# A matmul with 2:4-pruned weights: the first seven token tiles as runs of 128 neighbouring rows

## The chip, the core and the metric

The kernel runs on one core of a Trainium2 chip. Its matrix unit is TensorE (PE in the profile, with PEld for its weight loads); elementwise work is shared by VectorE (DVE), ScalarE (ACT) and GpSimd (POOL). Transfers are carried out by 16 DMA engines and are started by instructions on queues, here those of SyncE (SP) and of ScalarE. The metric is the device time of one execution in microseconds, as the median of several runs.

## The reference

x has 16 x 512 tokens of 1024 features, w is 1024 x 1024, b has 1024 entries; all are bfloat16. In every column of w, of each four neighbouring rows the two with the larger magnitude stay and the others become zero. Then x is multiplied by the pruned w, and b is added:

```python
wg = w.reshape(G, M, D)                  # M = 4
mag = jnp.abs(wg)
order = jnp.argsort(mag, 1)
thr = jnp.take_along_axis(mag, order[:, M - N:M - N + 1, :], 1)   # N = 2
mask = (mag >= thr)
wp = (wg * mask).reshape(D, D)
return jnp.einsum("bsd,df->bsf", x, wp) + b
```

## The kernel before

The 8192 tokens are 64 tiles of 128. For a tile, TensorE needs x with features on the partitions and tokens along the free dimension, as the stationary operand, and multiplies it with 512 columns of pruned weights at a time; eight blocks of 128 features are summed in one PSUM bank.

The weights are pruned on the chip. w_sb holds w in a layout in which one partition has the four rows of a group of four (w row g\*512 + 4q + m is at partition q, half g, slot m), so that VectorE can compare the four slots. Six pieces are pruned one after another: four of 256 columns of the upper half of the features (pieces 0 to 3), then two of 512 columns of the lower half (4, 5). The result is wp. For most tiles it is then spread by DMAs within the chip into wp_nat, where feature rows lie in their natural order (function spread, tokens W in the orders).

While that goes on, the first seven tiles (NPK = 7) are started early. Their upper 512 features (HK) are loaded untransposed by load_x (lines 105 to 110), in three transfers named by GROUPS: tile 6 alone on ScalarE's queue, tiles 3 to 5 and then 0 to 2 on SyncE's. TensorE transposes them against an identity (function transpose, line 198; in each tile four transposes, for the features of slot m), ScalarE copies the result to xt (line 203), and mm_piece (line 228) multiplies it with the pieces 0 to 3 of wp as they become ready. In these seven tiles a row on partition p and tile t of a group that starts at tile a is row a\*128 + 3p + t of x: function tokens gives that view, and three neighbouring rows of x are on one partition.

The lower 512 features of tiles 0 to 5 come later through two transposing DMAs into xlow (load_low, line 236). These take the 384 rows of a group in natural order, so the columns of a tile are every third one of xlow: the view xq. The sums of the upper half wait in a staging buffer st, to which GpSimd adds the bias; close then multiplies the lower half (function nat, line 242), VectorE adds st (line 429) and writes to o, and a store goes to the rows that rows names. Tiles 7 to 11 (xlead) and all later ones (xb, in batches of up to eight tiles) arrive by transposing DMAs and need neither the on-chip transposes nor tokens.

The order of work on each engine at the start is written out by hand in the table order, one list for each engine (T: transposes of a tile, C: copy, M: matmuls of a tile with a piece, S and U: staging copies, W, X, Y, Z: transfers, A and E: openings of later tiles). On TensorE all seven T stand ahead of the first M, in the order 6, 5, 3, 4, 2, 0, 1. On SyncE's queue the transfers of the start stand in this order: two slots of piece 0 of w; x tiles 3 to 5; x tiles 0 to 2; pieces 1, 2 and 3 of w; the first half of the lower w; then the transposing load of xlead. ScalarE's queue issues the other two slots of piece 0 and tile 6.

Of the kernel before, what the change touches and what calls it, by code (L numbers as in the profile page):

```python
# [10 lines left out]
def kernel(  # L11
# [8 lines left out]
    P = 128  # L20
# [14 lines left out]
    HK = D // G  # L35
    assert G == 2 and Dout == 2 * FH and HK == 512
    xf = x.flatten_outer_dims()
    of = out.flatten_outer_dims()

    NPK = 7  # L40
# [3 lines left out]
    GROUPS = ((0, 3), (3, 6), (6, 7))  # L44
# [21 lines left out]
    def seq(eng, inst):  # L66
        if eng in tails:
            tc.add_manual_dep(inst.ins, tails[eng].ins.name, NOSYNC, reason="program order")
        tails[eng] = inst
        return inst  # L70
# [10 lines left out]
    def sp(i):  # L81
        return seq("sp", i)
# [7 lines left out]
    wv = w.rearrange("(g q m) f -> q g m f", g=G, m=4)  # L90
    x_sb = {}
    
    def tokens(dram, t):
        a, b_ = next(s for s in GROUPS if s[0] <= t < s[1])
        return dram[a * P:b_ * P].rearrange("(p t) k -> p t k", p=P), t - a
    bias_sb = const.tile([P, Dout], bf16)

    def issue(eng, out_, in_):
        q = nc.sync if eng == "sp" else nc.scalar
        return seq(eng, q.dma_start(out_, in_))  # L100
# [3 lines left out]

    def load_x(ta, tb, eng="sp"):
        xs = const.tile([P, tb - ta, HK], bf16, name=f"x_{ta}")
        xv, n = tokens(xf, ta)
        issue(eng, xs[:], xv[:, n:n + tb - ta, :HK])
        for t in range(ta, tb):
            x_sb[t] = xs[:, t - ta, :]  # L110

# [10 lines left out]
    load_w(0, 0, 256, 0, 2)  # L122
    load_w(0, 0, 256, 2, 4, "act")
    load_x(SOLO, SOLO + 1, "act")
    act(nc.scalar.activation(spark[:], nc.const_aps.tensor(1.0, [P, 1], bf16), Act.Abs))
    load_x(3, 6)
    load_x(0, 3)
    load_w(0, 256, 512)
    load_w(0, 512, 768)
# [103 lines left out]
    def load_low(u):  # L233
        a, b_ = GROUPS[u]
        xlow = const.tile([P, 4, (b_ - a) * P], bf16, name=f"xlow{u}")
        sp(nc.sync.dma_start_transpose(out=xlow[:], in_=xf[a * P:b_ * P, HK:]))
        xq = xlow[:].rearrange("p k (q t) -> p k q t", t=b_ - a)
        return {a + t: xq[:, :, :, t] for t in range(b_ - a)}

    def nat(xt, ps, c0, c1, k0=0, k1=KT, first=0, last=KT - 1, koff=0):  # L240
        for kt in range(k0, k1):
# [48 lines left out]
    p = {}  # L290
# [53 lines left out]
    def emit(eng, tok):  # L344
# [10 lines left out]
        elif tok[0] == "Z":  # L355
            load_w(1, 512, 1024)
            sp(nc.sync.dma_start(bias_sb[:], b.partition_broadcast(P)))
        elif tok[0] == "X":
            xnat.update(load_lead(int(tok[1:])))
        elif tok[0] == "Y":  # L360
            xnat.update(load_low(int(tok[1:])))
        elif tok[0] == "E":
            open_solo(int(tok[1:]))
        elif tok[0] == "U":
            t, h = map(int, tok[1:].split("h"))
            stage((t, "h", h))
        elif tok[0] == "A":
            open_nat(*map(int, tok[1:].split("h")))
        elif tok[0] == "C":
            copy_xt(int(tok[1:-1]))  # L370
        elif tok[0] == "M":
            mm_piece(*map(int, base[1:].split(".")), part[k])
        elif tok[0] == "S":
            stage(tuple(map(int, tok[1:].split("b"))))
        else:
            i = int(base[-1])
            if i not in p:
                p[i] = Piece(i)
            if eng == "act":
                p[i].abs_act()  # L380
            else:
                p[i].do(base[:-1], part[k], half.get(k, slice(0, 2)))
# [47 lines left out]
                                        ps.rearrange("p (n c) -> p n c", n=2), add, op=Alu.add))  # L430

    def rows(t):
        if t < NPK:
            ov, n = tokens(of, t)
            return ov[:, n, :]
        return of[t * P:(t + 1) * P, :]

    def store(eng, t, o, c0=0, c1=Dout):
        issue(eng, rows(t)[:, c0:c1], o[:, c0:c1])
# [25 lines left out]
    for bi, (tb, nb) in enumerate(batches):  # L465
        if bi:
            load_batch(bi + 1)
        for j in range(nb):
            t = tb + j
# [49 lines left out]
```

## Time and profile before

| | |
|---|---|
| median of 3 runs | 234.71 us (234.15 to 235.56) |
| the profiled execution | 236.29 us |
| its span, first to last instruction | 234.5 us |
| its mean granted TensorE clock | 0.993 |
| DMA packets, bytes | 79260, 38.19 MB |
| x tiles 0 to 5, untransposed | two transfers of 384 KB |

The page gives busy times of the engines and the chain of work that ended last, followed back from the last instruction. Views of the trace give the chain's pieces in order of time (start, length, what), who waited for whom, groups of instructions with their count and mean duration, and busy times in stretches that one can choose. In the timeline a line gives start, length, engine, line of the kernel, operation, tiles and count. SPq and ACTq are the issuing instructions on the queues; a DMA's own time runs from its issue to its landing.

### The profile page before, as it was taken

To read this page: it belongs to the slowest core of one execution; us is meant where nothing else is said; L and a number is where in the kernel's file an instruction comes from. 1 tells how busy PE (TensorE), PEld (TensorE's weight loads), DVE (VectorE), ACT (ScalarE), POOL (GpSimd) and SP (SyncE) were. 2 spreads that over 40 slices of the span, in tenths; PEclk is the share of its full clock that TensorE was granted. 3 is DMA by queue.
4 is the path that set the end of the run, shared out by engine and by line. 5 is a ranking of instruction groups with operands and counts; after the bars stand their busy time and mean duration, and the time that the engine had idled before them with its cause. 6 is when DMAs were issued, how large, how long until landed. Compare 5 with 4: busy or idle time off the path is not lost.

```text
span 234.5 us, 2804 instructions
## 1 busy us (share of the span) xinstructions
PE 227.3 (97%) x1124; PEld 111.6 (48%) x1144; DVE 107.8 (46%) x191; ACT 14.4 (6%) x27; POOL 17.6 (7%) x15
## 2 busy tenths in 40 slices
PE   6799999999999999999999999999999999999995
PEld 3688444444444444444444444444444444444443
DVE  4599957882442442343344244234334324423434
ACT  3575200000000000000000000000000000000000
POOL 1000079900000000000000000000000000000000
PEclk9799999999999999999999999999999999999999
DMA  5988999997279312992219912594227931222122
GB/s 151 291 171 241 245 189 232 272 327 265 89 168 306 129 69 89 192 282 108 92 59 260 262 63 74 127 307 149 92 89 159 285 137 60 77 89 89 48 89 89
DMA packets 79260, 38.19 MB, mean 163 GB/s; under 512 B 64144, under 2 KB 71696, under 8 KB 79248
## 3 DMA queue, kind: packets, MB, share of 16 engines
q1 hardware_dynamic: 68464, 20.88, 41.6%
q10 hardware_dynamic: 10784, 17.14, 20.5%
q8 instruction: 9, 0.15, 0.3%
q14 instruction: 3, 0.02, 0.0%
HBM read 3.28 MB, written 16.78 MB: 86 GB/s over the span
## 4 chain that ended last, share of the span: by engine, by line
PE 95%; DMA 3%; issue 1%; SPq 0%; DVE 0%
PE ps L242 87%; PE ps L228 5%; DMA x<-in_x_dram 3%; PE tp L242 2%; SPq L100 0%; PE tp L198 0%; PE ps L198 0%; DVE o L427 0%
## 5 line engine op out<-in xcount | busy, mean ns | idle before, releaser
L242 PE MATMUL ps<-wp_nat,xb 128*128 128x512 bf16 (+1 forms) x831 | 178.9, 375 | 0.9
L242 PEld LDWEIGHTS <-xb 128*128 128x128 bf16 x848 | 82.4, 98 | 97.5
L427 DVE TENSOR_TENSOR o<-ps,bias_sb 128x512 bf16<-128x512 f32 (+1 forms) x112 | 71.5, 676 | 114.5 <-PE ps L242 112.2
L423 POOL TENSOR_TENSOR st<-st,bias_sb 128x1024 f32<-128x1024 f32 x8 | 16.7, 2124 | 0.0
L242 PE MATMUL ps<-wp_nat,xlead 128*128 128x512 bf16 x63 | 14.7, 379 | 0.1
L242 PEld LDWEIGHTS <-xlead 128*128 128x128 bf16 x88 | 8.6, 98 | 10.2
L228 PE MATMUL ps<-wp,xt 128*128 128x256 bf16 x112 | 12.7, 277 | 0.0
L429 DVE TENSOR_TENSOR o<-ps,st 128x512 bf16<-128x512 f32 x16 | 11.1, 691 | 2.8 <-PE ps L242 2.0
L228 PEld LDWEIGHTS <-xt 128*128 128x128 bf16 x112 | 11.2, 100 | 1.4
L242 PE MATMUL ps<-wp_nat,xlow 128*128 128x512 bf16 x47 | 10.6, 379 | 0.1
L264 ACT COPY st<-ps 128x512 f32<-128x512 f32 x14 | 7.3, 596 | 3.9 <-PE ps L228 3.8
L242 PEld LDWEIGHTS <-xlow 128*128 128x128 bf16 x48 | 5.0, 103 | 5.4
L162 DVE TENSOR_TENSOR wp<-w_sb,mag 128x256 bf16<-128x256 bf16 (+2 forms) x13 | 6.1, 480 | 0.1
L162 DVE TENSOR_TENSOR mag<-mag,hi 128x256 bf16<-128x256 bf16 (+2 forms) x13 | 6.0, 482 | 0.2
L242 PE MATMUL tp<-wp_nat,xlead 128*128 128x512 bf16 x23 | 5.8, 379 | 0.0
L172 DVE TENSOR_SCALAR mag<-w_sb 128x512 uint16<-128x512 uint16 (+2 forms) x5 | 2.3, 476 | 6.0 <-DMA w_sb<-in_w_dram 6.0
L198 PE MATMUL tp<-ident,x 128*128 128x128 bf16 x20 | 2.4, 283 | 2.6 <-DMA x<-in_x_dram 2.6
L141 PE MATMUL ps<-const-bfloat16-1.0 128*128 128x128 bf16 (+1 forms) x20 | 3.8, 366 | 0.8 <-PEq L503 0.8
L198 PEld LDWEIGHTS <-x 128*128 128x128 bf16 x28 | 2.6, 138 | 3.0 <-DMA x<-in_x_dram 3.0
L141 PEld LDWEIGHTS <-const-bfloat16-1.0 128*128 128x128 bf16 x20 | 1.9, 126 | 2.4 <-issue 2.4
L162 DVE TENSOR_TENSOR lo<-mag 128x512 bf16<-128x512 bf16 (+1 forms) x6 | 3.1, 509 | 0.1
L162 DVE TENSOR_TENSOR hi<-mag 128x512 bf16<-128x512 bf16 (+1 forms) x6 | 3.0, 508 | 0.1
(18 smaller groups left out, 17.1 us busy)
## 6 DMA issues: line engine op xcount, KB each, us to landing
out_dram<-o ACTq DMA_DIRECT2D x58, 256.0 KB, 2.0
wp_nat<-wp SPq DMA_DIRECT2D x14, 128.0 KB, 3.3
out_dram<-o ACTq DMA_DIRECT2D x10, 128.0 KB, 1.7
w_sb<-in_w_dram SPq DMA_DIRECT2D x2, 512.0 KB, 6.0
x<-in_x_dram SPq DMA_DIRECT2D x2, 384.0 KB, 6.3
w_sb<-in_w_dram SPq DMA_DIRECT2D x3, 256.0 KB, 7.1
bias_sb<-in_b_dram SPq DMA_DIRECT2D x1, 256.0 KB, 4.2
wp_nat<-wp ACTq DMA_DIRECT2D x2, 128.0 KB, 3.1
```

Of the source, the lines that this page charges most:

```text
L141: pe(nc.tensor.matmul(warm_ps[:, :rep * P], lhsT=nc.const_aps.tensor(1.0, [P, P], bf16), rhs=nc.const_aps.tensor(1.0, [P, rep * P], bf16), ...
L162: dve(nc.vector.tensor_tensor(out, a, b_, op=op))
L172: dve(nc.vector.tensor_single_scalar(self.mag[:, ms, :].bitcast(u16), self.w[:, ms, :].bitcast(u16), 0x7FFF, op=Alu.bitwise_and))
L198: pe(nc.tensor.transpose(tp[:, m, :], xg[:, m, :], ident[:]))
L228: pe(nc.tensor.matmul(ps[:, c0 + d:c1 + d], lhsT=xpk[t][:, m, :], rhs=wp[:, g, m, c0:c1], start=(new and m == ms.start), stop=(left[key] = ...
L242: pe(nc.tensor.matmul(ps, lhsT=xt[:, kt - koff, :], rhs=wp_nat[:, kt, c0:c1], start=(kt == first), stop=(kt == last)))
L264: act(nc.scalar.copy(staged[(q, h)][:, at, :, :].rearrange("p t c -> p (t c)"), ps_open.pop(key)[:]))
L423: pool(nc.gpsimd.tensor_tensor(st[:], st[:], bias.to_broadcast([P, 2, 2, CW]), op=Alu.add))
L427: dve(nc.vector.tensor_tensor(o[:, c0:c1], ps, bias_sb[:, c0:c1], op=Alu.add))
L429: dve(nc.vector.tensor_tensor(o[:, c0:c1].rearrange("p (n c) -> p n c", n=2), ps.rearrange("p (n c) -> p n c", n=2), add, op=Alu.add))
```

## The change

All tiles are 128 neighbouring rows of x, with row p on partition p. load_x still loads three tiles with one DMA, now with the view "(t p) k -> p t k" of the 384 rows, and a partition's three pieces are row p of three tiles. xlow's columns of a tile are a contiguous run of 128. Output tiles 0 to 5 are stored to 128 neighbouring rows, as the others were. The function tokens is gone. Tile 6 is as it was.

```diff
-    def tokens(dram, t):
-        a, b_ = next(s for s in GROUPS if s[0] <= t < s[1])
-        return dram[a * P:b_ * P].rearrange("(p t) k -> p t k", p=P), t - a
     def load_x(ta, tb, eng="sp"):
         xs = const.tile([P, tb - ta, HK], bf16, name=f"x_{ta}")
-        xv, n = tokens(xf, ta)
-        issue(eng, xs[:], xv[:, n:n + tb - ta, :HK])
+        issue(eng, xs[:], xf[ta * P:tb * P, :HK].rearrange("(t p) k -> p t k", p=P))
...
         sp(nc.sync.dma_start_transpose(out=xlow[:], in_=xf[a * P:b_ * P, HK:]))
-        xq = xlow[:].rearrange("p k (q t) -> p k q t", t=b_ - a)
-        return {a + t: xq[:, :, :, t] for t in range(b_ - a)}
+        return {a + t: xlow[:, :, t * P:(t + 1) * P] for t in range(b_ - a)}
...
     def rows(t):
-        if t < NPK:
-            ov, n = tokens(of, t)
-            return ov[:, n, :]
         return of[t * P:(t + 1) * P, :]
```

## The prediction

> **What bounds the kernel now.** I read the page's busy line and chain first, then the chain in order of time.
>
> ```profile
> PE 227.3 (97%) x1124; PEld 111.6 (48%) x1144; DVE 107.8 (46%) x191; ACT 14.4 (6%) x27; POOL 17.6 (7%) x15
> PE 95%; DMA 3%; issue 1%; SPq 0%; DVE 0%
> ...
> 1.24 0.67 SPq L100
> ...
> 1.97 6.74 DMA x<-in_x_dram
> 8.71 0.05 issue
> 8.75 1.04 PE tp L198 x8
> 9.80 0.43 PE ps L198 x4
> 10.22 12.53 PE ps L228 x112
> 22.75 0.86 PE tp L242 x4
> ...
> 229.57 2.16 PE ps L242 x25
> ```
>
> The chain ends in TensorE and stays on it without a break from 8.75 us to the last matmul at 229.57 + 2.16 = 231.7 us. That work is the same before and after, so time can be won or lost in two ways only: TensorE starts its unbroken run at another moment, or a new hole opens in it. What sets the start is one transfer: the second three-tile load of x (tiles 0 to 2), issued at 1.97 and landed at 8.71. It is one of the transfers that the diff rewrites. The waits say the same:
>
> ```profile
> DVE mag L172 <- DMA w_sb<-in_w_dram: 6.0, 2, 3.3
> PE tp L198 <- DMA x<-in_x_dram: 2.6, 2, 2.4
> ```
>
> TensorE waits for data only twice, both times for x. VectorE waits for w, which is queued behind x on the same queue. So I looked at what the DMA engines did meanwhile (columns: stretch; length, then busy time of PE, PEld, DVE, ACT, POOL; PEclk; DMA share; GB/s).
>
> ```profile
> 1.50:2.50 1.00, 1.00 (x4) 0.36 (x3) 0.00 (x0) 0.71 (x1) 0.00 (x0) 1.00 0.44 121
> 2.50:3.50 1.00, 1.00 (x5) 0.44 (x4) 0.21 (x1) 0.78 (x2) 0.00 (x0) 1.00 1.08 303
> 3.50:4.50 1.00, 1.00 (x17) 1.00 (x16) 0.97 (x4) 0.00 (x0) 0.00 (x0) 1.00 0.59 136
> 4.50:5.50 1.00, 0.27 (x5) 0.11 (x2) 0.93 (x5) 0.37 (x1) 0.00 (x0) 1.00 0.90 257
> 5.50:6.50 1.00, 0.00 (x0) 0.00 (x0) 1.00 (x5) 0.00 (x0) 0.00 (x0) 1.00 0.78 214
> 6.50:7.50 1.00, 0.38 (x5) 0.39 (x6) 0.43 (x2) 0.00 (x0) 0.00 (x0) 0.90 0.98 289
> 7.50:8.50 1.00, 0.99 (x10) 0.72 (x7) 0.00 (x0) 0.74 (x2) 0.00 (x0) 0.50 1.14 347
> ...
> 9.80:22.75 12.95, 12.95 (x117) 11.46 (x116) 12.54 (x39) 8.99 (x17) 0.00 (x0) 0.97 0.96 220
> ```
>
> The reader is to see a hole: 303 GB/s while the first w pieces and tile 6 come in, 136 when the x loads begin, 347 only after 7.5. With five loads already issued the DMA engines were not full: something fed them too slowly. Against 347 GB/s the five stretches from 2.5 to 7.5 lack 44 + 211 + 90 + 133 + 58 = 536 KB, which is 1.54 us of transfer.
>
> **The change, part by part.** *The three-tile loads.* Bytes (384 KB), count (three pieces of 1 KB to each of 128 partitions), queue and place in it stay. What changes is the list of source rows. Before, 3p+t over all p and t is 384 evenly spaced rows, one plain count, while the destination is 128 partitions of three pieces: the two sides step unlike. After, the source is 128 rows, each with jumps of 128 rows, which cannot be one count: both sides are 128 by 3. The trace has loads of both kinds. Alike: the first w pieces (two of every four rows), tile 6, the stores. Unlike: the x loads, the four-row w pieces, the spreads into wp_nat.
>
> ```profile
> 0.73 0.45 SPq L100 DMA_DIRECT2D w_sb<-in_w_dram  x1
> 1.24 1.33 SPq L100 DMA_DIRECT2D x<-in_x_dram  x2
> 2.61 4.26 SPq L100 DMA_DIRECT2D w_sb<-in_w_dram  x4
> 0.74 0.50 ACTq L100 DMA_DIRECT2D w_sb<-in_w_dram  x1
> 1.26 0.49 ACTq L100 DMA_DIRECT2D x<-in_x_dram  x1
> ...
> L100 SPq DMA_DIRECT2D x<-in_x_dram x2: 604/639/674, 1.2 to 2.0; - x2
> L100 SPq DMA_DIRECT2D wp_nat<-wp x14: 542/604/1322, 13.2 to 32.9; - x14
> L100 ACTq DMA_DIRECT2D out_dram<-o x70: 338/338/817, 40.8 to 232.1; - x70
> L357 SPq DMA_DIRECT2D bias_sb<-in_b_dram x1: 637/637/637, 17.2 to 17.2; - x1
> DMA to landing us min/median/max: 2.6/5.8/6.7
> ```
>
> Alike issues cost 0.34 to 0.50 us, unlike ones about 0.6 (the bias, alike and 0.64, is an exception). The last line is of x: tile 6, alike, landed 2.6 us after its issue; the three-tile loads, with three times the bytes, took 5.8 and 6.7. I read the hole as the unlike loads being prepared too slowly to fill the engines. The trace bears that out only in part, since those loads are also the bigger ones.
>
> Bounds. Least: nothing but the issue is shorter, twice 0.64 - 0.45 = 0.19, so the second load starts 0.37 us earlier. Most: the engines run full. Up to the end of the second x load 128 + 128 + 128 + 384 + 384 KB = 1.18 MB must move; 0.12 MB was moved by 2.5; 1.06 MB at 347 GB/s is 3.05 us, so 5.55. To that comes the lag to landing: tile 6 landed at 1.26 + 2.6 = 3.86, while its 0.39 MB (it and the two w pieces) had moved by about 3.4, so 0.46. Landing at 6.0 instead of 8.71 is 2.7 us.
>
> *Does the rest follow?* VectorE's pruning is the other input of the matmuls from 10.02 on.
>
> ```profile
> 6.32 0.62 DVE L162 TENSOR_TENSOR wp<-w_sb,mag 128x256 bf16<-128x256 bf16 x2
> 9.62 0.43 DVE L172 TENSOR_SCALAR mag<-w_sb 128x1024 uint16<-128x1024 uint16 x1 [2.69 <-DMA w_sb<-in_w_dram]
> 12.01 0.28 DVE L162 TENSOR_TENSOR wp<-w_sb,mag 128x256 bf16<-128x256 bf16 x1
> 15.14 0.42 DVE L162 TENSOR_TENSOR wp<-w_sb,mag 128x512 bf16<-128x512 bf16 x1
> ```
>
> Piece 0 is finished at 6.94; piece 1 starts at 9.62 when its 256 KB of w land, and VectorE is then busy in a row. Full engines would bring that w at 5.55 + 0.76 + 0.46 = 6.8, so piece 1 starts at 6.94, 2.68 earlier. TensorE takes 12.53 / 4 = 3.13 us for each of the four pieces; it needs piece 1 at 10.22 + 3.13 = 13.35, which is ready at 12.29, and piece 2 at 16.48, ready at 15.56: 0.9 us to spare. So VectorE lets 2.7 through. Later waits hang on the same VectorE chain and move with it.
>
> Which value? The w loads behind x still step unlike, and may now be what leaves the engines empty. I give back half of the 1.54 us: gain 2.7 - 0.8 = 1.9 us, nearer to the upper end because the alike loads at 2.5 to 3.5 did fill the engines.
>
> *Row distance.* The three pieces of a partition now lie 256 KB apart instead of 2 KB. No row shows that. Bounds: nothing, as the stores' pitch of 6 KB or 2 KB hardly matters here; and a loss as in the slower rival below. I take nothing.
>
> The Trainium skill speaks against the change here: "DMA: Bandwidth & Descriptors", section Latency and other measured facts, gives 207 GB/s at a per-partition pitch of 512 KiB against 214 unhindered, and far less from 2 MiB on. Taken at its worst for half that pitch, an estimate of 3% on 6.74 us, that would be 0.2 us; no run here shows it yet.
>
> *xlow, xpk and the rest.* The stationary operand of tiles 0 to 5 in the second half is read with a step of three elements before, without one after:
>
> ```profile
> L242 PEld LDWEIGHTS <-xlow 128*128 128x128 bf16 x48 | 5.0, 103 | 5.4
> L242 PEld LDWEIGHTS <-xlead 128*128 128x128 bf16 x88 | 8.6, 98 | 10.2
> 38.99 2.75 PE L242 MATMUL ps<-wp_nat,xlead 128*128 128x512 bf16 x12
> 41.58 1.03 PE L242 MATMUL tp<-wp_nat,xlead 128*128 128x512 bf16 x4
> 44.17 7.93 PE L242 MATMUL ps<-wp_nat,xlow 128*128 128x512 bf16 x35
> 51.94 4.26 PE L242 MATMUL ps<-wp_nat,xb 128*128 128x512 bf16 x19
> ```
>
> Weight loads shrink from 103 to 98 ns, but they lie under the matmuls: 36 xlow matmuls (one record missing) from 44.17 to 51.94 are 216 ns each, 12 xlead ones from 38.99 to 41.58 also 216. Worth 0; uncovered it would be 48 x 5 ns = 0.24. The two transposing loads into xlow have the same source and destination. The on-chip transposes read tiles of the same form. The six output tiles go to contiguous rows instead of every third; ScalarE's queue issues them while TensorE is never held, so 0.
>
> *Sum.* Span 234.5, less 1.9, is 232.6. The profiled execution took 236.29, 1.79 outside its span and 1.58 above the median of the runs, 234.71; taking the change off that median gives **232.8 us**.
>
> **The rivals.** *Nothing but the issue* (20%): the hole comes from the size of the three-tile loads or from the start of the program, and stays. For it: they are the biggest early loads. Against it: 347 GB/s is reached with unlike w loads in flight, so size alone doesn't hold the engines down. Then 0.37 off: 234.3.
>
> *The clock takes it back* (8%). PEclk is 0.50 in 7.5 to 9.5, after the stretches 4.5 to 7.5 in which TensorE was busy for 0.65 us; from 9.8 to 22.75 it is 0.97. With x earlier, the half-speed stretch of some 2.5 us may fall on the 112 matmuls instead of on the transposes, half of it lost: 1.9 - 1.25 = 0.65 off, 234.1. Against it: the idle stretch itself shrinks. The Trainium skill ("TensorE: Matmul & The Clock Gate", Part 1) says the clock comes back after about 3.4 us of sustained work; by that the cost is at most an estimated 1.7 us, and the trace's stretch agrees roughly.
>
> *The reads get slower* (16%): single rows from three places 256 KB apart come in more slowly than neighbours. The two loads move 0.79 MB between about 3.2 and 8.7, 143 GB/s; a quarter less would be 1.8 us more, all of it on the chain because TensorE and, through the w behind it, VectorE wait: 236.5. It decides from a loss of about 18% on (1.2 us). For it: the rate now is low and sensitive to something. Against: tile 6 and w are read with quite different row distances, at full rate.
>
> **How the numbers follow.** Forecast 56%, the rivals 20, 8 and 16. A measurement here can tell 0.5% (1.17 us) from no change. The forecast's own range is gains of 1.2 to 2.7, 232.0 to 233.5; all of it is faster. The two middle rivals are within 0.5%, 28%; the last is slower, 16%. The range goes from full engines plus half a microsecond of scatter, 231.5, to no change plus the same scatter, 235.3; the slower rival is left out of it.
>
> **What would show it.** Right: issues of x near 0.45 us; 3.5 to 5.5 us at 300 GB/s or more; the chain's x step ending near 6 to 7 instead of 8.71; piece 1 on VectorE starting near 7 to 8; the 112 matmuls starting near 8; 216 ns for xlow matmuls. Wrong: issues still 0.6 us; the 136 GB/s hole unchanged; x landing after 8.7; or the hole moved to w, so that VectorE starts piece 1 at 9.6 as before and TensorE gets breaks at L228, which would leave 0.9 us of gain at most.

## The result, and the profile after

| | before | changed |
|---|---|---|
| median (18 executions each) | 235.59 us (234.15 to 237.21) | 233.66 us (233.50 to 234.62) |
| ratio, 95% interval | | 0.9926 (0.9905 to 0.9947) |
| span of the profiled execution | 234.5 us | 232.1 us |
| mean granted TensorE clock in it | 0.993 | 0.999 |

The kernel became faster by 0.74%, which is 1.74 us between the means; the medians are 1.93 us apart. The change moves tiles 0 to 5; tile 6, a group of one tile, was a run of 128 neighbouring rows before as well. Not only the median moved: the executions of the kernel before are spread over 3 us, those of the changed one over 1.1 us.

The chain that ended last, in order of time, of the changed kernel (start, length, what; lines have moved up by three to five):

```profile
0.78 4.21 PE ps L137 x20
4.99 0.89 PE tp L194 x8
5.88 0.03 issue
5.91 0.59 PE tp L194 x4
6.51 0.02 issue
6.53 0.66 ACT xt L199 x2
7.18 0.64 PE tp L194 x8
7.82 0.22 PE ps L194 x4
8.05 12.32 PE ps L224 x112
20.37 0.86 PE tp L237 x4
```

The DMA step of 6.74 us is gone from it. The chain now starts with TensorE's first matmuls, which multiply constants (L137), and goes straight on to the transposes; the only thing between them is a copy by ScalarE. The 112 matmuls start at 8.05 instead of 10.22. The issues and landings of x (timeline of SyncE's queue, then two lines of the view of tile x):

```profile
1.24 0.99 SPq L97 DMA_DIRECT2D x<-in_x_dram  x2
2.27 2.68 SPq L97 DMA_DIRECT2D w_sb<-in_w_dram  x4
...
L97 SPq DMA_DIRECT2D x<-in_x_dram x2: 457/469/481, 1.2 to 1.8; - x2
DMA to landing us min/median/max: 3.5/3.8/5.4
```

Two issues take 0.99 us instead of 1.33. Tiles 3 to 5 land at 1.24 + 3.8 = 5.0 (before, 1.24 + 5.8, by unrounded times about 7.1), tiles 0 to 2 at 7.1 instead of 8.7. The stretches of the changed kernel (length, busy time of PE, PEld, DVE, ACT, POOL, then PEclk, DMA share, GB/s):

```profile
2.50:3.50 1.00, 1.00 (x5) 0.44 (x4) 0.13 (x1) 0.78 (x2) 0.00 (x0) 1.00 1.14 372
3.50:4.50 1.00, 1.00 (x12) 1.00 (x11) 0.97 (x4) 0.00 (x0) 0.00 (x0) 1.00 0.99 324
4.50:5.50 1.00, 1.00 (x12) 0.88 (x11) 0.93 (x5) 0.01 (x1) 0.00 (x0) 1.00 0.92 254
5.50:6.50 1.00, 0.97 (x12) 0.80 (x10) 1.00 (x5) 0.73 (x2) 0.00 (x0) 1.00 0.84 238
6.50:7.50 1.00, 0.53 (x10) 0.38 (x8) 0.50 (x2) 0.65 (x2) 0.00 (x0) 1.00 1.13 341
7.50:8.50 1.00, 1.00 (x16) 0.87 (x13) 0.42 (x1) 0.86 (x3) 0.00 (x0) 1.00 1.16 317
```

Two things are to be seen. The hole of 136 GB/s at 3.5 to 4.5 is filled, and a shallower one (254, 238) follows where the second x load is under way. And the clock column is 1.00 throughout: before, it was 0.50 from 7.5 to 9.5.

### The profile page after: what moved, and what is told of

It is laid out like the page before. It is cut to its first block, busy times and chain, and to the rows that moved or that the text cites. A ratio compares the mean times of both kernels' runs of the same rounds, so it can differ in the third digit from the quotient of the medians.

```text
span 232.1 us, 2824 instructions
## 1 busy us (share of the span) xinstructions
PE 228.1 (98%) x1144; PEld 110.8 (48%) x1144; DVE 107.8 (46%) x191; ACT 14.2 (6%) x27; POOL 17.6 (8%) x15
## 4 chain that ended last, share of the span: by engine, by line
PE 98%; ACT 0%; DVE 0%; issue 0%
PE ps L237 88%; PE ps L224 5%; PE tp L237 2%; PE ps L137 2%; PE tp L194 1%; ACT xt L199 0%; DVE o L422 0%; PE ps L194 0%
## 5 line engine op out<-in xcount | busy, mean ns | idle before, releaser
L237 PE MATMUL ps<-wp_nat,xb 128*128 128x512 bf16 (+2 forms) x848 | 179.8, 375 | 0.0
L237 PEld LDWEIGHTS <-xlead 128*128 128x128 bf16 x88 | 8.6, 98 | 10.2
L224 PEld LDWEIGHTS <-xt 128*128 128x128 bf16 x112 | 10.7, 98 | 1.5 <-ACT xt L199 0.2
L137 PE MATMUL ps<-const-bfloat16-1.0 128*128 128x128 bf16 (+1 forms) x20 | 4.2, 405 | 0.8 <-PEq L495 0.8
L137 PEld LDWEIGHTS <-const-bfloat16-1.0 128*128 128x128 bf16 x20 | 2.3, 143 | 2.4 <-issue 2.4
```

Of the source, the lines that this page charges most:

```text
L137: pe(nc.tensor.matmul(warm_ps[:, :rep * P], lhsT=nc.const_aps.tensor(1.0, [P, P], bf16), rhs=nc.const_aps.tensor(1.0, [P, rep * P], bf16), ...
L224: pe(nc.tensor.matmul(ps[:, c0 + d:c1 + d], lhsT=xpk[t][:, m, :], rhs=wp[:, g, m, c0:c1], start=(new and m == ms.start), stop=(left[key] = ...
L237: pe(nc.tensor.matmul(ps, lhsT=xt[:, kt - koff, :], rhs=wp_nat[:, kt, c0:c1], start=(kt == first), stop=(kt == last)))
```

## The experiments

All run beside the kernel before on the same chip. "x(3..5)" is the landing of the first three-tile load in the profiled execution, its issue plus its time to landing; "GB/s" is the DMA rate from 3.5 to 4.5 us there; "below full clock" counts the executions whose mean granted clock was under 0.997, nearly all of them 0.991 to 0.993. Landing and rate are of one execution each: e8 changes nothing in the transfers of the kernel before, and has 6.6 us and 170 GB/s where that has 7.1 and 136, so differences of this size say nothing.

| | x(3..5) us | GB/s | below full clock | median us | ratio (95%) |
|---|---|---|---|---|---|
| before, all 107 beside the experiments | 7.1 | 136 | 51 of 107 | 235.74 | 1 |
| changed | 5.0 | 324 | 0 of 18 | 233.66 | 0.9926 (0.9905 to 0.9947) |
| e1, neighbours, slots walked backwards | 7.2 | 177 | 6 of 12 | 235.87 | 1.0001 (0.9971 to 1.0032) |
| e2, changed, no flag | 6.1 | 225 | 6 of 12 | 235.71 | 0.9997 (0.9967 to 1.0027) |
| e5, neighbours, flagged | 5.1 | 356 | 0 of 7 | 233.82 | 0.9926 (0.9896 to 0.9955) |
| e6, w in pairs | 5.3 | 343 | 2 of 12 | 234.13 | 0.9939 (0.9911 to 0.9967) |
| e7, x issued 0.5 us later | 7.0 | 124 | 9 of 12 | 236.17 | 1.0007 (0.9979 to 1.0035) |
| e8, before, TensorE kept busy | 6.6 | 170 | 0 of 12 | 234.95 | 0.9977 (0.9953 to 1.0002) |
| e9, second x load without flag | 5.0 | 346 | 0 of 8 | 233.86 | 0.9930 (0.9902 to 0.9958) |
| e10, first x load without flag | 6.7 | 140 | 8 of 12 | 235.93 | 1.0009 (0.9979 to 1.0038) |
| e11, before, tile 6 later | 6.5 | 145 | 7 of 12 | 235.52 | 0.9989 (0.9962 to 1.0016) |
| e12, x and tile 6 later | 6.5 | 168 | 8 of 12 | 235.59 | 0.9990 (0.9963 to 1.0017) |
| e13, tile 6 first | 5.4 | 345 | 2 of 12 | 234.19 | 0.9937 (0.9904 to 0.9969) |
| e14, e7 with w in pairs | 6.7 | 81 | 6 of 12 | 236.37 | 1.0032 (1.0001 to 1.0062) |

### What in the load does it: rows, sides or flag

The built programs show one more thing that the diff does not say. The builder sets a flag for a shorter issue on a load whose two sides have the same counts and none of whose steps goes backwards. The three-tile loads carry it after the change and not before; the first w pieces, tile 6 and the stores carry it in both. (The bias load carries it too and took 0.64 us to issue, so the flag does not make every issue short.) So three properties changed at once: which rows are read, whether the two sides step alike, and the flag. Three kernels separate them.

e1, on the kernel before:

```diff
-        issue(eng, xs[:], xv[:, n:n + tb - ta, :HK])
+        issue(eng, xs[:, ::-1, :], xv[:, n:n + tb - ta, :HK][:, ::-1, :])
```

> The kernel before (rows 3p+t), but the two three-tile loads walk their three slots backwards on both sides: the same bytes go to the same places, and the source can no longer be one count of 384 rows, so both sides are 128 by 3. The builder sets its flag for the short issue only on loads whose steps all rise, so these stay without it. If it is enough that the two sides step alike: x(0..2) lands near 7.1 us and the time is about 0.993 of before. If the flag decides: issue about 0.6 us, landing near 8.7, ratio 1.00. If the distance of the rows decides (neighbouring rows come in slowly): also 1.00.

e2, on the changed kernel:

```diff
+        nc.dge_precook = tb - ta < 3
         issue(eng, xs[:], xf[ta * P:tb * P, :HK].rearrange("(t p) k -> p t k", p=P))
+        nc.dge_precook = True
```

> The changed kernel with the builder's flag held back on the two three-tile loads alone; rows, both sides 128 by 3 and everything else as in the changed kernel. If the flag decides: issues of 0.6 us again, the hole of 136 GB/s at 3.5 to 4.5 us is back, x(0..2) lands at 8 to 9 us, ratio about 1.00. If the alike sides or the distance of the rows decide: as the changed kernel, landing 7.1, ratio 0.993.

e5, on the changed kernel (the upper features of tiles 0 to 5 are those of other tokens):

```diff
-        issue(eng, xs[:], xf[ta * P:tb * P, :HK].rearrange("(t p) k -> p t k", p=P))
+        issue(eng, xs[:], (xf[ta * P:(ta + 4) * P, :HK].rearrange("(p t) k -> p t k", t=4)[:, :3] if tb - ta == 3 else
+            xf[ta * P:tb * P, :HK].rearrange("(t p) k -> p t k", p=P)))
```

> The changed kernel, but the two three-tile loads fetch rows 4p, 4p+1, 4p+2 of a run of 512, so a partition has three neighbouring rows as before, and the load keeps its flag and its 128 by 3 form. The upper half of the features of tiles 0 to 5 then belongs to other tokens; the work is the same. If the form of the load decides: issues 0.47, x(0..2) lands near 7.1, ratio 0.993. If it is the distance of the rows: as before, landing near 8.7, ratio 1.00.

The x issues in e1, e2 and e5, in this order, from the view of tile x of each:

```profile
L100 SPq DMA_DIRECT2D x<-in_x_dram x2: 612/670/727, 1.2 to 2.0; - x2
```

```profile
L97 SPq DMA_DIRECT2D x<-in_x_dram x2: 612/668/724, 1.2 to 2.0; - x2
```

```profile
L97 SPq DMA_DIRECT2D x<-in_x_dram x2: 456/468/481, 1.2 to 1.7; - x2
```

Neighbouring rows with the flag have the whole gain (0.9926, the same as the changed kernel); the changed rows without the flag have none of it (0.9997), nor have alike sides without the flag (1.0001). Row distance and the form of the sides are worth nothing that these intervals (about 0.3% to either side) can show; the flag decides. e2 also keeps the contiguous xlow and the contiguous stores of the changed kernel, and stays at 0.9997: these two are worth nothing measurable.

### Which load, and how the flag acts

e9 and e10 hold the flag back on one of the two loads (tiles 0 to 2, or tiles 3 to 5), by the line of e2 with ta != 0 or ta != 3 in place of the condition.

> The changed kernel with the flag held back on the second three-tile load (tiles 0 to 2) alone. If each unflagged load is fed slowly by itself: x(3..5) lands near 5.0 as in the changed kernel and x(0..2) at 7.5 to 8.5, and since the chain hangs on the second, most of the gain is lost: ratio 0.997 to 1.000. If only the first load of a run of loads matters (empty DMA engines): as the changed kernel, ratio 0.993.

> The changed kernel with the flag held back on the first three-tile load (tiles 3 to 5) alone. If each unflagged load is fed slowly by itself and holds what is behind it: x(3..5) lands at 6 to 7, x(0..2) right behind it, 0.5 to 1 us later than in the changed kernel, ratio 0.995 to 0.998. If only the second load counts: ratio 0.993.

The stretch in question of e9, then of e10:

```profile
3.50:4.50 1.00, 1.00 (x12) 1.00 (x11) 0.97 (x4) 0.00 (x0) 0.00 (x0) 1.00 1.02 346
```

```profile
3.50:4.50 1.00, 1.00 (x17) 1.00 (x16) 0.97 (x4) 0.00 (x0) 0.00 (x0) 1.00 0.65 140
```

The gain hangs on the first of the two loads alone. In e9 the second is issued without the flag and lands at 7.0 all the same: my expectation that each unflagged load is fed slowly by itself was wrong.

e7 keeps the flag and moves the loads:

```diff
+    late = const.tile([P, 16], bf16)
+    issue("sp", late[:], xf[SOLO * P:NPK * P, :16])
     load_x(3, 6)
```

> The changed kernel with one more small flagged load (128 rows of 32 bytes, used by nobody) ahead of the two x loads on SyncE's queue, so that x and all of w behind it are issued about 0.5 us later, which is at least the 0.4 us that the unflagged issues cost. If the issue time alone is what the flag saves: this gives back nearly all of the 1.75 us, ratio about 0.999. If the flag matters for how quickly the pieces reach the DMA engines after the issue: over 300 GB/s at 3.5 to 4.5 us stay, at most 0.5 us is given back, ratio about 0.994 to 0.995.

```profile
1.24 0.45 SPq L97 DMA_DIRECT2D late<-in_x_dram  x1
1.74 0.96 SPq L97 DMA_DIRECT2D x<-in_x_dram  x2
...
3.50:4.50 1.00, 1.00 (x12) 1.00 (x11) 0.95 (x4) 0.00 (x0) 0.00 (x0) 1.00 0.64 124
```

(timeline of SyncE's queue and a stretch of e7). Both theories missed a part. The issues are as short as in the changed kernel (0.96 for two), and yet the hole of the kernel before is back and all of the gain is gone. So the flag alone does not keep the DMA engines busy. The loss is not the length of the delay either: 0.5 us more at the issue costs 7.0 - 5.0 = 2 us at the landing. What e7 does not tell apart is the delay and the load that makes it: x is issued later, and 128 pieces of 32 bytes now stand ahead of it on its queue.

e11, e12 and e13 ask whether the first x load must come ahead of tile 6 on the other queue. e11 puts a small load ahead of tile 6 in the kernel before, e12 the same in e7, e13 exchanges tile 6 and the w load ahead of it in the changed kernel:

```diff
+    late6 = const.tile([P, 16], bf16)
+    issue("act", late6[:], xf[3 * P:4 * P, :16])
     load_x(SOLO, SOLO + 1, "act")
```

> The kernel before, with one small flagged load (32 bytes of 128 rows, used by nobody) ahead of tile 6 on ScalarE's queue, so that tile 6 is issued at about 1.75 us instead of 1.26 and the three-tile load of SyncE, issued from 1.24 to 1.91 without the flag, is no longer behind it. If what the flag won is the place ahead of tile 6: tile 6 lands after 4.4 instead of 3.8, x(3..5) near 5 to 5.5 instead of 7, no execution at a clock of 0.993, ratio 0.994 to 0.996. If the place does not matter: x(3..5) at 6 to 7, executions at both clocks, ratio 1.00.

> The kernel with x and w issued 0.5 us later (which lost the whole gain, ratio 1.0007), and tile 6 now later by the same small load on ScalarE's queue, so that the flagged x(3..5) and tile 6 stand to each other as in the changed kernel. If the place relative to tile 6 decides: x(3..5) lands at 5 to 5.6, full clock, ratio 0.994 to 0.996. If it is the moment of issue: x(3..5) near 7 again, ratio 1.00.

> The changed kernel with the two loads of ScalarE's queue exchanged: tile 6 at 0.74 us, the second half of piece 0 of w at 1.26. Issue of x(3..5) stays at 1.24 with its flag. Half of piece 0 then comes later, so VectorE starts its first piece up to 1 us later, most of it on the chain. If the place relative to the second load of ScalarE's queue is what matters, whichever it is: x(3..5) still lands near 5.0 and TensorE has tiles 3 to 5 transposed by 6.5. If it must be ahead of tile 6 itself: x(3..5) at 6 to 7.

The place relative to tile 6 does not decide. With tile 6 behind x in e11 and e12 tiles 3 to 5 land at 6.5, ratios 0.999, no gain that the intervals tell from none; with tile 6 wholly ahead in e13 they land at 5.4 and the gain is there. That tile 6 lay behind them in the changed kernel was no cause. The ratios of e11 and e12 by themselves say little about x, because the small load also holds up tile 6, which TensorE transposes first: issued 0.5 us later, it lands at 1.78 + 4.42 = 6.2 in e11 and at 6.0 in e12, instead of 1.26 + 2.6 = 3.9.

e6 and e14 flag the w loads behind x too, by loading pieces 1 to 3 in pairs of slots, in the changed kernel and in e7:

```diff
-    load_w(0, 256, 512)
+    load_w(0, 256, 512, 0, 2)
+    load_w(0, 256, 512, 2, 4)
```

> The changed kernel with pieces 1 to 3 of w loaded as two loads of two slots each, so that these are flagged too (six issues of 0.45 instead of three of 0.62). In the changed kernel 254 and 238 GB/s remain at 4.5 to 6.5 us. If the unflagged w loads behind x leave the engines empty: over 300 GB/s there, x(0..2) lands near 6.0 instead of 7.14, a further gain of up to 1 us, ratio near 0.989. If the hole belongs to the second x load itself: landing stays 7.1, ratio 0.993; if the three more issues delay the lower w and the transposing load behind them, slower than the changed kernel by up to 0.8 us.

> The kernel with x issued 0.5 us later by a small load ahead of it (which lost the whole gain, 124 GB/s at 3.5 to 4.5 us), and pieces 1 to 3 of w in pairs of slots, so that every load up to the lower w is flagged. If what slows the feed is unflagged loads being prepared behind x: over 300 GB/s at 3.5 to 4.5, x(3..5) lands near 5.5 instead of 7, full clock, ratio 0.994 to 0.996. If it is that x reaches the DMA engines after they have run empty: the hole at 3.5 to 4.5 stays, x(3..5) near 7, executions at both clocks, ratio 1.00.

Stretches of e6, then of e14:

```profile
3.50:4.50 1.00, 1.00 (x12) 1.00 (x11) 0.97 (x4) 0.00 (x0) 0.00 (x0) 1.00 1.09 343
4.50:5.50 1.00, 1.00 (x11) 0.69 (x10) 0.93 (x5) 0.00 (x0) 0.00 (x0) 1.00 1.00 307
5.50:6.50 1.00, 0.99 (x13) 0.78 (x11) 1.00 (x5) 0.82 (x3) 0.00 (x0) 1.00 1.07 328
```

```profile
2.50:3.50 1.00, 1.00 (x5) 0.44 (x4) 0.23 (x1) 0.77 (x2) 0.00 (x0) 1.00 1.19 290
3.50:4.50 1.00, 1.00 (x12) 1.00 (x11) 0.96 (x4) 0.00 (x0) 0.00 (x0) 1.00 0.60 81
4.50:5.50 1.00, 0.91 (x9) 0.64 (x7) 0.93 (x5) 0.05 (x1) 0.00 (x0) 1.00 0.91 235
```

e6 closes the second hole, over 300 GB/s all the way, and tiles 0 to 2 land at 6.7 instead of 7.1 in its profiled execution. It brings nothing that can be measured, 0.9939 against 0.9926; in the changed kernel there were only 0.6 us of waiting for x left to win. In e14 every load ahead of the lower w is flagged, and with x half a microsecond late the hole is the deepest of all, 81 GB/s. Unflagged loads behind x do not make it. (e14 is a little slower than the kernel before, 1.0032, with an interval that just leaves out 1.)

What the runs have in common is a condition: in every kernel in which the first x load is issued at 1.24 us with the flag, the DMA engines stay at 320 to 360 GB/s from 3.5 to 4.5 us and it lands by 5.4; in every other the rate falls to 80 to 225 there, and it lands at 6.1 or later.

The moment at which x reaches the engines does not explain it. The traces also record when each single piece of a transfer starts; pieces of 1 KB on SyncE's queue are those of x at this time. The first of them starts at 2.8 to 2.9 us in the changed kernel, e5, e6 and e9, but at 3.27 in e13, which has the gain as well; in the kernels without the gain it starts between 2.87 (e11) and 3.37 (e2), and at 3.16 in the kernel before. What divides them is how quickly the others follow: in the half microsecond after the first, 119 to 148 pieces of x start in the five kernels with the gain, and 23 to 82 in the nine without it (135 in the changed kernel, 47 in the one before, 40 in e7). Tile 6 is slow in the same way where the small load stands ahead of it: its 128 pieces start over 1.9 us in e11 and over 2.2 us in e12, against 0.5 in the kernel before.

In these runs, then, a flagged first x load is fed quickly from its start, and an unflagged one is not; and a flagged load behind the small one is fed slowly too. Whether the small load does this by the delay or by its own 128 pieces is not shown, since no run delays x in another way.

### The clock

e8, on the kernel before: in TensorE's order "T6a T5a" becomes "T6a F36 T5a", 36 matmuls of constants where it waits for x.

> The kernel before with 36 matmuls of constants on TensorE between the transposes of tile 6 and of tile 5, where it waits for x; they write a bank that nobody reads and end before x is there. Nothing else moves. If part of the gain is the clock, which was 0.50 in the transposes of the kernel before and 1.00 in the changed one: the twelve last transposes take 0.9 us instead of 1.5, the 112 matmuls never fall under full speed, and the time is 0.5 to 0.8 us below before, ratio about 0.997, without the runs above 236. If the clock is worth nothing: ratio 1.000; if the filler is in the way: slower.

All 12 executions have the full clock, and their median is 234.95, 0.23% below before (0.9977, interval to 1.0002). The transposes of x into tp, in the kernel before and then in e8 (shortest, median and longest in ns):

```profile
L198 PE MATMUL tp<-ident,x x20: 218/311/314, 4.4 to 9.5; 128*128 128x128 bf16 x20
L198 PE MATMUL tp<-ident,x x20: 216/218/315, 4.8 to 8.8; 128*128 128x128 bf16 x20
```

How long the clock is down is best seen in e10, where the stretches can be cut at its ends:

```profile
6.70:7.30 0.60, 0.54 (x10) 0.55 (x11) 0.24 (x1) 0.09 (x1) 0.00 (x0) 0.99 1.05 333
7.30:10.70 3.40, 3.38 (x26) 2.68 (x24) 1.89 (x7) 2.99 (x7) 0.00 (x0) 0.50 1.17 324
10.70:12.00 1.30, 1.30 (x14) 1.16 (x13) 1.30 (x6) 0.00 (x0) 0.00 (x0) 1.00 1.19 198
```

3.4 us at half speed, 1.7 us of clock, which is 0.7% of the span and thus the 0.993 of an execution. It hits half of the executions of the kernel before, 51 of 107. Their median is 236.19; the 56 at full clock have 234.82 (234.63 to 234.84 on the four chips). TensorE stands idle for about 2 us there until x is landed (2.35 us in the profiled execution); in the changed kernel it does not, and none of 18 is hit. That the idle time brings on the slow stretch is what e8 shows. How much of it is enough stays open: e6 and e13, whose profiled executions wait for x for at most 0.3 and 1.0 us at a time, had 2 of 12 each, and e5, with 1.2 us, none of 7.

## Why the prediction was right, and where it was off

**The bound.** Right. The start of TensorE's unbroken run was the one place to win: from 8.05 in the changed kernel, from 10.22 before, 2.2 of the 2.4 us between the two spans; the 112 matmuls took 12.32 instead of 12.53, the other 0.2.

**The issue.** Right in size: 0.19 us predicted for each, 0.64 - 0.47 = 0.17 measured, and it is the flag that e2 takes away.

**Why the hole was there.** The step "unlike loads are prepared too slowly to fill the engines" was half right. The first x load was indeed fed too slowly, 47 pieces in its first half microsecond against 135 after the change. But it is not the unlike sides that do it: with alike sides and no flag a hole is there too, if a shallower one (177 GB/s in e1, 225 in e2), and none of the gain. Nor is it a property of each unflagged load: behind a well-fed first load the unflagged second one lands at 7.0, the flagged one at 7.1 (e9 and the changed kernel). The prediction's least bound, 0.37 us for a shorter issue with the hole left as it was, has no run to it: wherever the first load has the short issue at 1.24 us, the hole is filled.

**The signs.** The issues (0.47), the matmuls (from 8.05) and piece 1 on VectorE came as foretold. Two signs came only in part: 300 GB/s or more was to hold from 3.5 to 5.5 us and held to 4.5 (324, then 254), and tiles 0 to 2 landed at 7.1, a little after the 6 to 7 of the forecast. The doubt for which the sum gave back 0.8 us, that the w loads behind x would leave the engines empty, is borne out: with these in flagged pairs (e6) the stretches from 4.5 to 6.5 us have 307 and 328 GB/s, in the four other kernels with the gain 212 to 285.

**The term of the sum.** The 1.9 us taken for the x load was mis-sized. At the same full clock, 234.82 against the changed kernel's 233.66 (all 18 full), it is worth 1.16 us. The other part is the clock, for which the sum had nothing: 51 of 107 executions lose 236.19 - 234.82 = 1.37 us, and getting rid of that is about 0.65 us of the mean. Together 1.8, against the measured 1.74. That the sum came out so near was luck in part: one term was taken too large, and one that it did not have made up for it.

**The clock as a rival** had the wrong sign, and its stretch was read too short: not 2.5 us but 3.4, as the mean clock of 0.55 from 7.0 to 10.2 us and 0.91 from 10.2 to 13.0 in the kernel before also gives. The earlier x does not push the half-speed stretch onto the matmuls; it takes away the idle time behind which the stretch comes. The Trainium skill ("TensorE: Matmul & The Clock Gate", Part 1) describes the window by which the clock is set as free-running, about 3.4 us long, and the number of slow matmuls as different from run to run. The 3.4 us at 0.50 and the half of the executions agree with it.

**Row distance.** To take nothing for it was right: 0.9926 with neighbours and with rows 256 KB apart. The estimate of 0.2 us from the Trainium skill ("DMA: Bandwidth & Descriptors", Latency and other measured facts) for large pitches does not show. The figure that the Trainium skill gives there is for the pitch from one partition to the next, while the 256 KB here lie between the pieces of one partition, so the runs neither bear it out nor speak against it.

**VectorE follows.** Right: it started piece 1 at 8.08, predicted near 7 to 8 (start, length, group; what ended its idle time):

```profile
8.08 0.43 DVE L168 TENSOR_SCALAR mag<-w_sb 128x1024 uint16<-128x1024 uint16 x1 [1.08 <-DMA w_sb<-in_w_dram]
```

and the 112 matmuls have no break in the chain.

**xlow.** Right: weight loads at 98 ns, matmuls as before.

```profile
L237 PEld LDWEIGHTS <-xlow 128*128 128x128 bf16 x48 | 4.7, 98 | 5.7
41.79 7.93 PE L237 MATMUL ps<-wp_nat,xlow 128*128 128x512 bf16 x36
49.56 2.75 PE L237 MATMUL ps<-wp_nat,xb 128*128 128x512 bf16 x12
```

From 41.79 to 49.56 36 of them are 216 ns each.

**The baseline.** The profiled execution of the kernel before (236.29) was one of those with the slow stretch, at 0.993. That is the greater part (1.37 us) of its 1.58 us above the median of the first three runs, which the sum passed over as an offset. And that median, 234.71, is near that of the executions at full clock (234.82), while 18 executions have 235.59. From 234.71 to the measured 233.66 it is 1.05 us, not 1.9, and so the predicted 232.8 was 0.9 us too low although the difference between the kernels came out near.

What stays open: why the pieces of an unflagged first load, and of a flagged one behind the small load, follow each other so slowly. The runs show the condition, not the mechanism.

## What to carry to other kernels

A load whose source rows fall into one even count while its destination is partitions by slots was issued 0.17 us slower here than the same load with rows that do not, and as the first large load its pieces also came more slowly; look at the durations of the issuing instructions, and choose the order of rows accordingly where it is free. At the start of a kernel a delay need not be worth its own length: half a microsecond at one issue, made by a small load ahead of it, cost 2 us at the landing here. When executions of one kernel spread by a per cent, look at the granted clock of each and at TensorE's idle stretches before explaining medians.

## What was not expected of the hardware

A three-tile load landed 3.8 us after its issue when issued at 1.24 us, and 5.25 us after it when the same load was issued at 1.74 behind a load of 4 KB. And an idle TensorE of about 2 us costs 3.4 us at half clock in about half of the executions, 1.37 us each, so that a filler of 36 matmuls without any use made the kernel before 0.23% faster, at the edge of what its interval tells from none.
